# Attention and gated MLP on one core: the first MLP stage's rectified values kept in PSUM

## The chip, the cores and the metric

The kernel runs on one core of one Trainium2 chip. The metric is the device time of one execution in microseconds (us), lower is better. Engines are named as in the profile: PE is TensorE, DVE is VectorE, ACT is ScalarE, POOL is GpSimd, SP is SyncE, which issues most DMA transfers. PE writes its results to PSUM, in banks of 128 partitions by 512 fp32 values; DVE and ACT read and write both PSUM and SBUF; POOL works in SBUF here.

## The reference

Two stages follow each other. First causal attention with a decay, for 8 batches of 8 heads, 576 tokens and a head width of 64:

```python
scores = scale * np.matmul(q, k.transpose(0, 1, 3, 2))
log_f = np.log(np.clip(f, 0.0001, 1.0))
cum = np.cumsum(log_f, axis=-1)
decay = cum[:, :, :, None] - cum[:, :, None, :]
scores = np.where(causal, -1000000000.0, scores + decay)
attn = np.exp(scores - max); attn = attn / (sum + 1e-09)
x = np.matmul(attn, v)          # 8 x 8 x 576 x 64, then to 8 x 576 x 512
```

Then a gated MLP with a product over the tokens:

```python
h = np.maximum(x @ w_in, 0.0)                 # 576 x 1024 per batch
u, v = h[..., :512], h[..., 512:]
v_n = (v - mean(v)) / np.sqrt(var(v) + 1e-06)   # over the 512 columns
v_s = np.einsum('ts,bsd->btd', w_spatial, v_n) + b_spatial[None, :, None]
out = (u * v_s) @ w_out
```

## The kernel before

All matrix products run on PE with operands split in two parts, a rounded high part and the low remainder, and three products in place of one; so nearly each PSUM result is copied by ACT into a high part, and DVE or POOL subtracts it to get the low part. Only the first five pairs of heads (P < NF) use plain fp32 operands in attention.

Attention goes by pairs of heads, four pairs to a batch. For a pair and head, `scores` makes four tiles of 128 queries in PSUM (`sc`), DVE adds the mask and takes the row maximum (L338), ACT takes the exponential into `tt` (L340), POOL divides by the sum (L348). `transposes` turns `tt` by PE into `tp` tiles (L394) and `evac` writes them as high and low part into `eh` and `el` (ACT L383, DVE L384). The last 64 queries of both heads run in one tile (`scores_tail`, L359, into `tl`) and `transposes_tail` turns five blocks of keys, three in a first `tp` tile and two in a second, the fourth block and the last 64 keys. For those last 64 keys, of which 64 partitions are a second copy, the low part is wanted in partitions 64 to 127 of the high tensor: L416 copies it there from the low tensor. `attend` multiplies with `v` into `x0` and `x1`, and ACT and DVE evacuate them to `xh` and `xl` (L442, L443, L445).

`moe(b)` takes a batch. Its first stage makes the normalised half `v_n`: for five blocks of tokens, i = 0 to 4, twelve matmuls (eight for the last block, whose 64 tokens stand twice) accumulate a tile `ps` of 128 by 512. ACT rectifies it (L533) into an SBUF tile `vx`, DVE takes statistics (L534, L535), POOL adds epsilon (L536) and raises to the power -0.5 (L537), DVE subtracts the mean and scales (L538), ACT rounds to the high part `vnh` (L540) and POOL subtracts for the low part `vnl` (L542). `vx` has two buffers, and a buffer is free again after L542. For the last block, ACT first copies the lower half to `vx` (L531) and DVE adds the upper half (L532). Further stages make `u` (eight accumulations, rectified by ACT at L563), the product over the tokens (eight accumulations, gated by DVE at L582) and the output product.

The accumulators come from `acc`: in batches 0 to 6 from the pool `ps_m` with two PSUM banks, in the last batch in turn from three pools of two banks each. A bank goes to a new accumulation when the last reader of the old one is through.

What sets the order: attention and the MLP are two generators. They are advanced in turn, attention ahead by a quarter of a batch, each by its own estimated cost. A scheduler then puts the instructions in an order for each engine by their dependences and by an estimate of times; on the chip each engine takes its own list strictly in that order and waits where an operand or a bank is not ready. So a changed dependence changes the order of all five lists.

Of the kernel before, what the change touches and what calls it, by code (L numbers as in the profile page):

```python
# [12 lines left out]
AF = mybir.ActivationFunctionType  # L13
ALU = mybir.AluOpType
# [5 lines left out]
NF = 5  # L20
NQ = 4
LEAD = 0.25
S = 576
D = 64
NB = 4
# [8 lines left out]
def f32(ap):  # L34
    return ap.bitcast(F32)
# [3 lines left out]
def attn_gmlp_kernel(ctx: ExitStack, tc: tile.TileContext, qk, v, f, w_in, w_sp, b_sp, w_out, out):  # L39
# [17 lines left out]
    V, A, G, T, SY = nc.vector, nc.scalar, nc.gpsimd, nc.tensor, nc.sync  # L57
# [20 lines left out]
    lnc = cst.tile([128, 3], F32, name="lnc")  # L78
# [175 lines left out]
    ET = {"f": cst.tile([128, 2, 1600], F32, name="ef", tag="eh")}  # L254
# [3 lines left out]
    def mm(o, l, r, st, sp):  # L258
        last['mm'] = T.matmul(o, l, r, start=st, stop=sp)  # L259
        return last['mm']  # L260
# [113 lines left out]

    nev = [0]

    def evac(P, ps, sel):
        if P < NF:
            (V.tensor_copy if nev[0] % 2 == 1 else A.copy)(sel(ET["f"]), ps)
            nev[0] += 1  # L380
            return
        h_ap, l_ap = sel(ET["h"]), sel(ET["l"])
        A.copy(h_ap, ps)  # L383
        V.tensor_tensor(out=l_ap, in0=ps, in1=f32(h_ap), op=ALU.subtract)  # L384

    def transposes(P, h):
        if P == NF and h == 0:
# [12 lines left out]
    def transposes_tail(P):  # L400
        def ev(e, off, step, n):
            return e[:, :, off:off + step * n].rearrange("p h (c s) -> p c h s", s=step)[:, :, :, 0:64]
        for cs, off, step in (((0, 1, 2), 512, 512), ((4, 3), 576, 640)):
            n = len(cs)
            tp = PS['t'].tile([128, 512], F32, name="tp")
            for j, c in enumerate(cs):
                T.transpose(out=tp[:, j * 128:(j + 1) * 128], in_=tl[:, c * 128:(c + 1) * 128], identity=ident)  # L407
            pv = tp[:, 0:128 * n].rearrange("p (c h s) -> p c h s", h=2, s=64)

            def dst(e):  # L410
                st = e[:, :, off:off + 64]
                return bass.AP(tensor=st.tensor, offset=st.offset,
                               ap=[list(st.ap[0]), [step, n], list(st.ap[1]), list(st.ap[2])])
            evac(P, pv, dst)
            if P >= NF and cs[0] == 4:
                V.tensor_copy(ET["h"][64:128, :, S:640], f32(ET["l"][64:128, :, S:640]))  # L416
            yield 107 * n

    def attend(P, h, xh, xl):
# [30 lines left out]
    def attention(b, ws=None):  # L450
        for P in range(b * PPB, (b + 1) * PPB):
# [27 lines left out]
            if nxt:  # L479
                yield from scores(P + 1, 0)  # L480
            yield from transposes_tail(P)
            if P + 2 < NPAIR:
                split(P + 2)
# [16 lines left out]
    def acc(b):  # L500

        nps[0] += 1
        pool, tag = ((ps_m, "ps"), (PS["t"], "tp"), (PS["s"], "sc"))[nps[0] % 3 if b == B - 1 else 0]
        return pool.tile([128, DM], F32, name=tag)

    def moe(b):
        X = [xs.pop(b * PPB + p) for p in range(PPB)]
        vh, vl = [], []
        for i in range(NB + 1):
            ps = acc(b)  # L510
            n = 0
            for p in range(PPB):
                xh, xl = X[p]
                if i < NB:
                    t = slice(128 * i, 128 * i + 128)
                    terms = ((xh[:, t], 0), (xh[:, t], 1), (xl[:, t], 0))
                else:
                    terms = ((xh[:, TL:640], 0), (xh[:, TL:640], 1))
                for l, r in terms:
                    mm(ps, l, win[p][:, r, :], n == 0, n == len(terms) * PPB - 1)  # L520
                    n += 1
                yield 648
            th = mo.tile([128, DM], F32R, name="vnh", tag="vnh", bufs=5)
            tlo = mo.tile([128, DM], F32R, name="vnl", tag="vnl", bufs=4) if i < NB else None
            x = mo.tile([128, DM], F32, name="vx", tag="vx", bufs=2)
            st = mo.tile([128, 6], F32, name="st", tag="st", bufs=2)
            mv = mo.tile([128, 2], F32, name="mv", tag="mv", bufs=2)
            m = slice(0, 128)
            if i == NB:
                m = slice(0, 64)  # L530
                A.copy(x[64:128, :], ps[64:128, :])  # L531
                V.tensor_tensor(out=x[m, :], in0=ps[m, :], in1=x[64:128, :], op=ALU.add)  # L532
            A.activation(x[m, :], ps if i < NB else x[m, :], AF.Relu)  # L533
            V.bn_stats(out=st[m, :], in_=x[m, :])  # L534
            V.bn_aggr(out=mv[m, :], in_=st[m, :])  # L535
            G.tensor_tensor(out=mv[m, 1:2], in0=mv[m, 1:2], in1=lnc[m, 0:1], op=ALU.add)  # L536
            G.tensor_tensor(out=mv[m, 1:2], in0=mv[m, 1:2], in1=lnc[m, 1:2], op=ALU.pow)  # L537
            V.tensor_scalar(out=x[m, :], in0=x[m, :], scalar1=mv[m, 0:1], scalar2=mv[m, 1:2],  # L538
                            op0=ALU.subtract, op1=ALU.mult)
            A.copy(th[m, :], x[m, :])  # L540
            if i < NB:
                G.tensor_tensor(out=tlo, in0=x, in1=f32(th[:]), op=ALU.subtract)  # L542
                vl.append(tlo)
            else:
                A.copy(vb_[m, :], x[m, :])
                G.tensor_tensor(out=th[64:128, :], in0=x[m, :], in1=f32(th[m, :]), op=ALU.subtract)
            vh.append(th)
            yield 0
        if b == 0:
            open_m2()  # L550
        us = {}
        for j in range(NJ):
            for t0, nt in HALVES:
                ps = acc(b)
                n = 0
                for p in range(PPB):
                    xh, xl = X[p]
                    for l, r in ((0, xh), (1, xh), (0, xl)):
                        mm(ps[:, 0:nt], win[NJ + j][:, l, 128 * p:128 * p + 128], r[:, t0:t0 + nt], n == 0, n == 3 * PPB - 1)
                        n += 1  # L560
                    yield 369
                us[j, t0] = m2[0].tile([128, 320], F32, name="u", tag="U", bufs=9)
                A.activation(us[j, t0][:, 0:nt], ps[:, 0:nt], AF.Relu)  # L563
        if b % 2 == 0:
            gt[0] = m2[0].tile([128, 2, NJ, 128], F32R, name="gt", tag="gt")
        r0 = 64 * (b % 2)
        for t0, nt in HALVES:
            gh, gl = [], []
            for j in range(NJ):
                ps = acc(b)  # L570
                o = ps[:, 0:nt]
                js = slice(128 * j, 128 * j + 128)
                for c in range(NB):
                    mm(o, vh[c][:, js], sph[c][:, t0:t0 + nt], c == 0, False)
                    mm(o, vh[c][:, js], spl[c][:, t0:t0 + nt], False, False)
                    mm(o, vl[c][:, js], sph[c][:, t0:t0 + nt], False, False)
                    yield 370
                mm(o, vh[NB][:, js], spta[:, t0:t0 + nt], False, False)
                mm(o, vb_[:, js], sptb[:, t0:t0 + nt], False, True)
                yield 246  # L580
                g = us[j, t0][:, 0:nt]
                V.tensor_tensor(out=g, in0=o, in1=g, op=ALU.mult)  # L582
                gh.append(m2[0].tile([128, 320], F32R, name="gh", tag="GH", bufs=3))
                gl.append(m2[0].tile([128, 320], F32R, name="gl", tag="U", bufs=9))
                A.copy(gh[j][:, 0:256], g[:, 0:256])  # L585
                G.tensor_tensor(out=gl[j][:, 0:256], in0=g[:, 0:256], in1=f32(gh[j][:, 0:256]), op=ALU.subtract)  # L586
                if t0:
                    th, tlo = (gt[0][:, r, j, r0:r0 + 64] for r in range(2))
                    A.copy(th, g[:, 256:320])
                    G.tensor_tensor(out=tlo, in0=g[:, 256:320], in1=f32(th), op=ALU.subtract)  # L590
            for c0 in (0, 128):
                yield from w_out_tile(b, [g[:, c0:c0 + 128] for g in gh], [g[:, c0:c0 + 128] for g in gl],
                                      [(b, t0 + c0, 0, 128)])
        if b % 2 == 1:
            yield from w_out_tile(b, *[[gt[0][:, r, j, :] for j in range(NJ)] for r in range(2)],
                                  [(b - 1, TL, 0, 64), (b, TL, 64, 64)])
# [50 lines left out]
    def open_m2():  # L647
        while need[0] != "m2":
            need[0] = next(wgen)
        late.close()  # L650
        m2.append(ctx.enter_context(tc.tile_pool(name="m2", bufs=1, reuse_waits="tile")))
        last["m2"] = None
        converted()
# [54 lines left out]
```

## Time and profile before

| what | value |
|---|---|
| time, median of 3 runs (lowest to highest) | 806.53 us (804.21 to 806.70) |
| time of the profiled execution | 803.75 us |
| its span in the profile | 802.0 us |
| granted TensorE clock, mean | 0.991 |
| instructions | 15504 |

The profile is of one execution. Busy time of an engine is time in which one of its instructions runs; the chain that ended last is found by going back from the last instruction to what released it. A group of instructions is given as line, engine, operation, out<-in with shapes, count, then busy us and mean ns of one, then the engine's idle time before it and what ended most of that. A stretch is given as from:to in us, its length, then PE, PE weight loads, DVE, ACT and POOL busy with counts, the granted clock, the share and rate of DMA. A line of the timeline is start, duration, engine, line, operation, tiles, and in brackets the engine's idle time just before it with what ended it. A wait is given as who waited and for whom, with its sum in us, the times, and the longest.

### The profile page before, as it was taken

The page shows a single profiled execution, that of the slowest core. Times are in us where ns is not written, and L with a number is a line of the kernel's source. Part 1 is how long each engine was busy: PE and PEld are TensorE (multiplying, and loading weights), DVE is VectorE, ACT ScalarE, POOL GpSimd, SP SyncE. Part 2 cuts the span into 40 slices and gives each one's busy share as a digit, 9 for nine tenths or more (in the row PEclk, how much of TensorE's full clock was granted, in tenths as well). Part 3 has the DMA queues.
Part 4 walks back from the last instruction along what each step waited for, and adds up shares of the span by engine and source line. Part 5 has one row for each costly group of instructions (what it writes and reads, how often), then busy time and mean ns, then how long its engine had stood idle before and what let it go on. Part 6 is the DMA issues. An engine that isn't in the chain of part 4 may idle for free.

```text
span 802.0 us, 15504 instructions
## 1 busy us (share of the span) xinstructions
PE 781.6 (97%) x4980; PEld 703.8 (88%) x4981; DVE 553.2 (69%) x1665; ACT 535.6 (67%) x1418; POOL 475.2 (59%) x660
## 2 busy tenths in 40 slices
PE   8997989989999999999999999999999999999997
PEld 4776879879899989989899989999899988999996
DVE  7887786985768768676776669666787558674421
ACT  7785677676777767766676668766687667664431
POOL 5775796766765548655656647555776447643251
PEclk9998999999999999999999999999999999999999
DMA  8839645564454664545545455564555464330001
GB/s 222 251 95 236 173 131 135 137 165 137 122 126 102 164 172 114 126 118 135 136 112 141 117 144 128 144 158 133 145 126 136 118 166 126 83 78 14 27 1 66
DMA packets 41713, 103.48 MB, mean 129 GB/s; under 512 B 6831, under 2 KB 8879, under 8 KB 41568
## 3 DMA queue, kind: packets, MB, share of 16 engines
q1 hardware_dynamic: 41306, 101.96, 49.6%
q8 instruction: 40, 0.66, 0.3%
q10 hardware_dynamic: 326, 0.53, 0.3%
q14 instruction: 41, 0.34, 0.1%
HBM read 39.42 MB, written 10.68 MB: 62 GB/s over the span
## 4 chain that ended last, share of the span: by engine, by line
PE 86%; POOL 4%; ACT 3%; DMA 2%; issue 2%; DVE 2%; POOLq 0%; ACTq 0%; DVEq 0%
PE ps L259 46%; PE sc L259 16%; PE x L259 13%; PE tp L394 8%; PE tp L259 2%; PE tp L407 2%; POOL tt L348 1%; POOL lo L279 1%; DMA tb<-lo 1%; DMA vraw<-in_dram 1%; ACT eh L383 1%; ACT tt L340 1%; POOL wa L171 0%; DMA out_dram<-o 0%; DMA ft<-in_dram 0%
## 5 line engine op out<-in xcount | busy, mean ns | idle before, releaser
L348 POOL TENSOR_SCALAR tt<-tt,sm 128x128 f32<-128x128 f32 (+3 forms) x256 | 141.9, 574 | 78.7 <-DVE sm L344 61.2
L338 DVE CUSTOM_DVE_ANT_0 tt<-sc,zm 128x128 f32<-128x128 f32 (+3 forms) x256 | 122.7, 486 | 91.4 <-PE tp L394 65.1
L383 ACT CAST eh<-tp 128x512 fp32r<-128x512 f32 (+1 forms) x270 | 111.3, 425 | 76.3 <-PE tp L394 50.1
L340 ACT ACTIVATE tt<-tt,nm 128x128 f32<-128x128 f32 (+3 forms) x256 | 144.3, 565 | 22.7 <-DVE nm L338 21.2
L384 DVE TENSOR_TENSOR el<-tp,eh 128x512 fp32r<-128x512 f32 (+1 forms) x270 | 126.7, 484 | 25.5 <-ACT eh L383 23.1
L394 PE MATMUL tp<-ident,tt 128*128 128x128 f32 x640 | 111.6, 279 | 3.2 <-DVE el L384 3.1
L259 PE MATMUL sc<-ta 128*128 128x128 f32 (+1 forms) x336 | 108.8, 330 | 1.9 <-DVE nm L338 1.6
L259 PE MATMUL sc<-tb 68*128 68x128 f32 (+1 forms) x336 | 105.8, 319 | 3.0 <-DMA tb<-lo 3.0
L259 PE MATMUL x<-eh,vt 128*128 128x320 f32 (+4 forms) x378 | 102.7, 286 | 0.4 <-POOL vt L315 0.4
L259 PE MATMUL ps<-xh,win 128*128 128x256 f32 (+1 forms) x464 | 99.0, 303 | 0.4 <-ACT u L563 0.3
L586 POOL TENSOR_TENSOR gl<-u,gh 128x256 fp32r<-128x256 f32 x64 | 47.3, 740 | 87.4 <-ACT gh L585 77.9
L279 POOL TENSOR_TENSOR lo<-raw,hi 128x640 fp32r<-128x640 f32 (+1 forms) x56 | 83.6, 1514 | 14.8 <-ACT hi L277 14.4
L259 PE MATMUL ps<-win,xh 128*128 128x512 f32 x296 | 91.6, 398 | 0.0
L259 PE MATMUL x<-el,vt 128*128 128x256 f32 x324 | 90.7, 304 | 0.2 <-DVE el L384 0.2
L394 PEld LDWEIGHTS tp<-ident,tt 128*128 128x128 f32 x640 | 76.5, 141 | 12.2 <-issue 2.3
L442 ACT CAST xh<-x 64x256 fp32r<-64x256 f32 (+1 forms) x128 | 49.7, 394 | 48.6 <-PE x L259 46.3
L259 PEld LDWEIGHTS ps<-xh,win 128*128 128x128 f32 x464 | 75.9, 191 | 2.1 <-ACT u L563 0.9
L259 PEld LDWEIGHTS x<-eh,vt 128*128 128x128 f32 x378 | 71.2, 189 | 3.3 <-POOL vt L315 1.0
L259 PE MATMUL ps<-sph,vnh 128*128 128x256 f32 (+1 forms) x240 | 73.2, 305 | 0.7 <-ACT o L611 0.7
L259 PE MATMUL ps<-wo,gh 128*128 128x512 f32 x224 | 72.1, 407 | 0.7 <-ACT wo L172 0.5
L443 DVE TENSOR_TENSOR xl<-x,xh 64x256 fp32r<-64x256 f32 (+1 forms) x128 | 57.5, 452 | 21.4 <-ACT xh L442 18.6
L259 PE MATMUL ps<-sph,vnl 128*128 128x256 f32 (+1 forms) x240 | 71.7, 299 | 0.0
(178 smaller groups left out, 1919.8 us busy)
## 6 DMA issues: line engine op xcount, KB each, us to landing
raw<-in_dram SPq DMA_DIRECT2D x28, 608.0 KB
ta<-hi SPq DMA_DIRECT2D x56, 304.0 KB
vraw<-in_dram SPq DMA_DIRECT2D x32, 320.0 KB
tb<-hi SPq DMA_DIRECT2D x56, 160.0 KB
ta<-lo SPq DMA_DIRECT2D x56, 160.0 KB
out_dram<-o SPq DMA_DIRECT2D x32, 256.0 KB
ta<-hi SPq DMA_DIRECT2D x56, 144.0 KB
tb<-lo SPq DMA_DIRECT2D x56, 144.0 KB
```

The lines of the kernel that those rows point to most:

```text
L259: last['mm'] = T.matmul(o, l, r, start=st, stop=sp)
L279: G.tensor_tensor(out=lo[:, c], in0=raw[:, c], in1=f32(hi[:, c]), op=ALU.subtract)
L338: V.tensor_tensor_reduce(out=t, in0=sc[:, 0:n], in1=zm[:, 640 - n:640], scale=-0.125, scalar=3.0e38, op0=ALU.add, op1=ALU.min, accum_out=n ...
L340: last["exp"] = last["exp", P, h, i] = A.activation(t, t, AF.Exp, bias=nm[:, i:i + 1], scale=-1.0, accum_out=se[:, i, 0:1])
L348: G.tensor_scalar(out=t, in0=t, scalar1=sm[:, i:i + 1], scalar2=1.0, op0=ALU.mult, op1=ALU.mult)
L383: A.copy(h_ap, ps)
L384: V.tensor_tensor(out=l_ap, in0=ps, in1=f32(h_ap), op=ALU.subtract)
L394: T.transpose(out=tp[:, (i - c) * 128:(i - c + 1) * 128], in_=tt[h][:, TOFF[i] + 128 * c:TOFF[i] + 128 * c + 128], identity=ident)
L407: T.transpose(out=tp[:, j * 128:(j + 1) * 128], in_=tl[:, c * 128:(c + 1) * 128], identity=ident)
L442: last[P, h] = A.copy(hi, ps[m0:m0 + 64, 0:n])
L443: V.tensor_tensor(out=lo, in0=ps[m0:m0 + 64, 0:n], in1=f32(hi), op=ALU.subtract)
L586: G.tensor_tensor(out=gl[j][:, 0:256], in0=g[:, 0:256], in1=f32(gh[j][:, 0:256]), op=ALU.subtract)
```

## The change

Three edits. First, in the MLP's first stage the rectified values are written back into the PSUM accumulator; statistics and normalisation read them there, and only the normalised values go to the SBUF tile `vx`. With it the bank's last reader is the normalisation, and the `vx` buffer is first written there and no longer by the Relu. Second, epsilon is added by DVE with a constant in place of POOL with a column of constants. Third, of the second tile of `transposes_tail` the fourth block's low part is subtracted into `el` as before, and that of the last keys is subtracted in place in partitions 64 to 127 of `eh`, so that L416 falls away; the first 64 partitions' low part of the last keys, which nothing reads, is no longer made.

```diff
-    def evac(P, ps, sel):
+    def evac(P, ps, sel, last_keys=False):
...
         A.copy(h_ap, ps)
-        V.tensor_tensor(out=l_ap, in0=ps, in1=f32(h_ap), op=ALU.subtract)
+        if last_keys:
+            V.tensor_tensor(out=l_ap[:, 1], in0=ps[:, 1], in1=f32(h_ap[:, 1]), op=ALU.subtract)
+            V.tensor_tensor(out=h_ap[64:128, 0], in0=ps[64:128, 0], in1=f32(h_ap[64:128, 0]), op=ALU.subtract)
+        else:
+            V.tensor_tensor(out=l_ap, in0=ps, in1=f32(h_ap), op=ALU.subtract)
...
-            evac(P, pv, dst)
-            if P >= NF and cs[0] == 4:
-                V.tensor_copy(ET["h"][64:128, :, S:640], f32(ET["l"][64:128, :, S:640]))
+            evac(P, pv, dst, cs[0] == 4)
...
-                V.tensor_tensor(out=x[m, :], in0=ps[m, :], in1=x[64:128, :], op=ALU.add)
-            A.activation(x[m, :], ps if i < NB else x[m, :], AF.Relu)
-            V.bn_stats(out=st[m, :], in_=x[m, :])
+                V.tensor_tensor(out=ps[m, :], in0=ps[m, :], in1=x[64:128, :], op=ALU.add)
+            A.activation(ps[m, :], ps[m, :], AF.Relu)
+            V.bn_stats(out=st[m, :], in_=ps[m, :])
             V.bn_aggr(out=mv[m, :], in_=st[m, :])
-            G.tensor_tensor(out=mv[m, 1:2], in0=mv[m, 1:2], in1=lnc[m, 0:1], op=ALU.add)
+            V.tensor_scalar(out=mv[m, 1:2], in0=mv[m, 1:2], scalar1=1.0e-6, scalar2=None, op0=ALU.add)
             G.tensor_tensor(out=mv[m, 1:2], in0=mv[m, 1:2], in1=lnc[m, 1:2], op=ALU.pow)
-            V.tensor_scalar(out=x[m, :], in0=x[m, :], scalar1=mv[m, 0:1], scalar2=mv[m, 1:2],
+            V.tensor_scalar(out=x[m, :], in0=ps[m, :], scalar1=mv[m, 0:1], scalar2=mv[m, 1:2],
```

In the changed file the first stage's Relu is L535, the statistics L536 and L537, the added epsilon L538, the power L539, the normalisation L540, and the last keys' two subtractions are L385 and L386.

The lists of the engines change with it. On PE, in batch 2's first stage, the third accumulation (ps_4020) follows the second (ps_3950) in the program before so; tp and sc, x0 and x1 are attention's transposes, scores and products with `v`:

```order
L259 MATMUL ps_3950<-win3_572,xh_3389 128x512 x2
L259 MATMUL ps_3950<-win3_572,xl_3390 128x512
L259 MATMUL x1_3830<-el_1228,vt_3551 128x192
L259 MATMUL x1_3830<-eh_1227,vt_3551 128x64
L394 MATMUL tp_3899<-ident_70,tt0_67 128x128 x3
L259 MATMUL ps_4020<-win0_235,xh_2417 128x512 x2
L259 MATMUL ps_4020<-win0_235,xl_2418 128x512
L259 MATMUL ps_4020<-win1_398,xh_2716 128x512 x2
L259 MATMUL sc_3932<-ta_3865 128x384
L259 MATMUL sc_3932<-tb_3866 128x384
```

Five matmuls of attention stand between the two, and the third accumulation is itself broken by scores. In the changed program the rows ahead of the third accumulation are these, and the second's last row is followed by three single matmuls (two of scores, one into x0) before they begin:

```order
L259 MATMUL sc_3811<-ta_3562 128x512
L259 MATMUL sc_3811<-tb_3563 128x512
L398 MATMUL tp_3776<-ident_70,tt1_68 128x128 x2
L259 MATMUL x0_3829<-el_1228,vt_3551 128x256
L259 MATMUL x0_3829<-eh_1227,vt_3551 128x128
L398 MATMUL tp_3784<-ident_70,tt1_68 128x128
L259 MATMUL x0_3829<-el_1228,vt_3551 128x128
L259 MATMUL x1_3830<-eh_1227,vt_3551 128x320
L259 MATMUL x1_3830<-el_1228,vt_3551 128x320
L259 MATMUL x1_3830<-eh_1227,vt_3551 128x320
L259 MATMUL x1_3830<-el_1228,vt_3551 128x320
L259 MATMUL ps_4020<-win0_235,xh_2417 128x512 x2
```

Fifteen matmuls of attention now stand between the two accumulations, and each accumulation runs unbroken. On DVE, the second group's statistics and normalisation (vx_4009, mv_4011) stood before among attention's evacuations like this:

```order
L534 BN_STATS st_4010<-vx_4009 128x6
L443 TENSOR_TENSOR xl_3714<-x1_3830,xh_3713 64x320
L535 BN_AGGR mv_4011<-st_4010 128x2
L445 TENSOR_TENSOR xl_3714<-x1_3830,xl_3714 64x320
L384 TENSOR_TENSOR el_1228<-tp_3899,eh_1227 128x384
L338 ISA tt0_67,nm_3917<-sc_3932,zm_77 128x384
L338 ISA nm_3917 128x1
L538 TENSOR_SCALAR vx_4009<-vx_4009,mv_4011 128x512
```

In the changed program the same group's end stands so on DVE, with the third group's statistics right behind the normalisation:

```order
L537 BN_AGGR mv_4011<-st_4010 128x2
L388 TENSOR_TENSOR el_1228<-tp_3776,eh_1227 128x256
L388 TENSOR_TENSOR el_1228<-tp_3784,eh_1227 128x128
L445 TENSOR_TENSOR xl_3714<-x0_3829,xh_3713 64x256
L538 TENSOR_SCALAR mv_4011<-mv_4011 128x1
L343 TENSOR_REDUCE sm_3789<-se0_107 128x4
L447 TENSOR_TENSOR xl_3714<-x0_3829,xl_3714 64x256
L344 RECIPROCAL sm_3789<-sm_3789 128x4
L540 TENSOR_SCALAR vx_4009<-ps_3950,mv_4011 128x512
L536 BN_STATS st_4071<-ps_4020 128x6
```

The epsilon row is new on DVE and the normalisation reads the accumulator ps_3950.

## The prediction

> **What bounds the kernel now.** I read the page first, for the busy shares and the chain that ended last; then the waits of TensorE; then busy time by stretch; then the groups by line and shape; last the timeline around the edited lines.
>
> ```profile
> span 802.0 us, 15504 instructions
> PE 781.6 (97%) x4980; PEld 703.8 (88%) x4981; DVE 553.2 (69%) x1665; ACT 535.6 (67%) x1418; POOL 475.2 (59%) x660
> PE 86%; POOL 4%; ACT 3%; DMA 2%; issue 2%; DVE 2%; POOLq 0%; ACTq 0%; DVEq 0%
> ```
>
> TensorE (PE) is busy for 97% of the span and carries 86% of the chain; it idles 802.0 - 781.6 = 20.4 us in all. The edit removes no matmul, so it can only move what lies in those 20.4 us, or add to them. Where they lie is told by stretches (after each engine's busy time, the granted clock):
>
> ```profile
> 80.00:130.00 50.00, 47.85 (x279) 41.49 (x278) 36.81 (x107) 34.17 (x86) 41.81 (x50) 0.97 0.59 157
> 130.00:200.00 70.00, 65.97 (x425) 59.19 (x424) 55.00 (x162) 49.64 (x135) 46.11 (x58) 0.98 0.54 138
> 410.00:470.00 60.00, 60.00 (x407) 56.31 (x406) 38.83 (x125) 38.22 (x107) 29.24 (x44) 1.00 0.55 144
> 775.00:802.00 27.00, 21.96 (x115) 18.91 (x113) 3.78 (x8) 5.02 (x14) 7.12 (x12) 0.98 0.14 49
> 290.00:320.00 30.00, 30.00 (x186) 27.14 (x186) 24.54 (x68) 22.17 (x56) 18.91 (x28) 1.00 0.50 125
> ```
>
> The first batch's MLP (80 to 130) leaves 2.2 us idle, the next stretch 4.0, the end 5.0. In the middle nothing is left: 60.00 of 60.00, and also 30.00 of 30.00 in 290 to 320, which is a first MLP stage, the part that is edited. There TensorE starts a matmul every 30.00 / 186 = 0.161 us. Of TensorE's waits, those that VectorE ended are the ones that this change can shorten:
>
> ```profile
> PE tp L394 <- DVE el L384: 3.1, 3, 2.1
> PE sc L259 <- DVE nm L338: 1.6, 4, 0.8
> PE tp L407 <- DVE el L384: 0.8, 1, 0.8
> ```
>
> Together 5.5 us. No row has the Relu (L533) or the normalisation (L538) as releaser: the stage's chain is today fully covered.
>
> **The parts on VectorE and GpSimd.** The rows of the edited lines, and of the nearest operations, by shape:
>
> ```profile
> L538 DVE TENSOR_SCALAR vx<-vx,mv 128x512 f32<-128x512 f32 x32 | 21.8, 683 | 5.1 <-POOL mv L537 4.2
> L538 DVE TENSOR_SCALAR vx<-vx,mv 64x512 f32<-64x512 f32 x8 | 7.1, 890 | 3.2 <-POOL mv L537 3.2
> L534 DVE BATCH_NORM_STATS2 st<-vx 128x6 f32<-128x512 f32 x32 | 21.6, 686 | 6.2 <-ACT vx L533 6.1
> L384 DVE TENSOR_TENSOR el<-tp,eh 128x512 fp32r<-128x512 f32 x54 | 37.1, 686 | 6.8 <-ACT eh L383 6.1
> L384 DVE TENSOR_TENSOR el<-tp,eh 128x256 fp32r<-128x256 f32 x81 | 33.9, 418 | 7.7 <-ACT eh L383 7.4
> L384 DVE TENSOR_TENSOR el<-tp,eh 128x128 fp32r<-128x128 f32 x54 | 15.2, 282 | 3.2 <-ACT eh L383 3.1
> L416 DVE CAST eh<-el 64x128 fp32r<-64x128 f32 x27 | 10.8, 400 | 0.9
> L365 DVE TENSOR_SCALAR sm<-sm 128x1 f32<-128x1 f32 x32 | 4.8, 149 | 4.8 <-ACT tl L364 4.3
> L536 POOL TENSOR_TENSOR mv<-mv,lnc 128x1 f32<-128x1 f32 x32 | 6.7, 214 | 49.3 <-DVE mv L535 30.6 <-DVE sm L343 18.7
> L536 POOL TENSOR_TENSOR mv<-mv,lnc 64x1 f32<-64x1 f32 x8 | 1.5, 182 | 6.6 <-DVE mv L535 4.1 <-DVE sm L344 2.4
> L533 ACT ACTIVATE vx<-ps 128x512 f32<-128x512 f32 x29 | 17.1, 597 | 7.9 <-POOL vnl L542 4.0 <-PE ps L259 3.8
> ```
>
> Last keys: 27 pairs lose a 128x256 subtraction (418 ns) and the copy (400) and get two subtractions of 128 columns, one on 64 partitions; both at the 128x128 row, 282. That is 27 x (818 - 564) = 6.9 us less VectorE time. Epsilon: 40 additions leave GpSimd (6.7 + 1.5 = 8.2 us) and come to VectorE at L365's 149 ns: 40 x 0.149 = 6.0 us more. It also takes one hand-over between engines out of the chain, since the addition now follows the aggregation on the same engine.
>
> Normalisation from PSUM: no tensor_scalar of that shape from PSUM is in the trace. The bounds are L538's own best, 518 ns, and L384's 686, which reads PSUM for the same 512 columns; the second is nearer and I take it.
>
> ```profile
> L538 DVE TENSOR_SCALAR vx<-vx,mv x40: 518/547/1897, 99.1 to 769.3; 128x512 f32<-128x512 f32 x32, 64x512 f32<-64x512 f32 x8
> 303.60 3.15 POOL L279 TENSOR_TENSOR lo<-raw,hi 128x640 fp32r<-128x640 f32 x2
> 303.67 1.79 DVE L538 TENSOR_SCALAR vx<-vx,mv 128x512 f32<-128x512 f32 x1 [0.17 <-POOL mv L537]
> ```
>
> An undisturbed L538 gets slower by 686 - 547 = 0.14 us, but the source view's maximum of 1897 ns, and the 1.79 us beside a long GpSimd subtraction, show what it suffers today; if that goes with the second operand in PSUM, 40 x 0.686 = 27.4 us stand against today's 21.8 + 7.1 = 28.9. So between +5.6 and -1.5 us; I take -1.5. The Trainium skill, "VectorE: DVE Perf Modes", section "Why PSUM operands drop a tier", says that the doubled fp32 rate needs both SBUF read ports and that PSUM offers one, which speaks against this part of the change: by it the 0.14 us is the whole story, and VectorE's sum would be 5.6 us up on this line. The trace agrees as far as its undisturbed rows go (547 against 686).
>
> Statistics from PSUM: L534 already takes 686, the same as a PSUM read of that width, so zero, 0.1 us either way. The Relu's destination: no ScalarE row that writes PSUM exists; L533's 597 is the nearest, 0.1 us either way, 40 x 0.1 = 4 us on an engine that is 67% busy. VectorE in sum: -6.9 + 6.0 - 1.5 = -2.4 us of 553; GpSimd -8.2 of 475. None of this is on TensorE, and matmuls cover it; what can come through is the stretch from 130 to 200, where VectorE is busy 55.00 of 70 and ends TensorE's waits: 27 pairs over some 690 us put 2.7 pairs there, 2.7 x 0.254 = 0.7 us. I credit -0.7.
>
> **The part on TensorE: the bank is held longer.** This is the term that counts. Today an accumulation's bank is free after the Relu; afterwards only after the normalisation, with GpSimd's power in between. Two banks serve the stage, so accumulation i+2 waits for the normalisation of i. Batch 2's first group, from its last matmul to the third group's first:
>
> ```profile
> 293.55 0.39 PE L259 MATMUL ps<-win,xl 128*128 128x512 f32 x1
> 294.78 0.58 ACT L533 ACTIVATE vx<-ps 128x512 f32<-128x512 f32 x1
> 297.30 0.56 POOL L537 TENSOR_TENSOR mv<-mv,lnc 128x1 f32<-128x1 f32 x1
> 297.89 0.60 DVE L538 TENSOR_SCALAR vx<-vx,mv 128x512 f32<-128x512 f32 x1
> 299.64 0.71 PE L259 MATMUL ps<-win,xh 128*128 128x512 f32 x2
> ```
>
> The chain takes 298.49 - 293.94 = 4.55 us and the third group comes 5.7 us after the first: it would fit even unmoved. A long case, batch 4's fourth group:
>
> ```profile
> 483.09 0.48 PE L259 MATMUL ps<-win,xl 128*128 128x512 f32 x1
> 487.13 0.60 ACT L533 ACTIVATE vx<-ps 128x512 f32<-128x512 f32 x1 [1.34 <-POOL vnl L542]
> 494.04 0.55 DVE L538 TENSOR_SCALAR vx<-vx,mv 128x512 f32<-128x512 f32 x1
> ```
>
> Here it takes 494.59 - 483.57 = 11.0 us. The new order answers by moving attention matmuls in between. Counted in it, from the end of one accumulation to the start of the next but one: 48, 44, 35 and 53 matmuls for batch 2's first four groups (38, 22, 24 and 27 before), the same four counts for batch 4, and 30 as the least in any batch. At 0.161 us each that is 7.7, 7.1, 5.6 and 8.5 us, and 4.8 at the least. The short chain is covered with 3 us to spare; the long one is late by 11.0 - 8.5 = 2.5 us. But 1.34 us of it was the Relu waiting until GpSimd had released the SBUF tile (row above), and in the change the Relu writes no such tile: 1.2 us remain. That SBUF wait is not abolished: it moves to the normalisation on VectorE, with the score reductions and evacuations queued behind it, and transposes and scores wait for those; it lies some 3 us later in the chain, by when GpSimd is through, so I cost it at zero (1.34 us a time if not).
>
> One group late in this way in all seven gated batches together makes +1.2 us. The sum against the profiled execution's own time: 803.75 + 1.2 - 0.7 = 804.25 us. That execution lies 806.53 - 803.75 = 2.78 us under the median of the runs shown, so the forecast on the median's footing is 807.0 us, within 0.3% (2.4 us, about what a measurement of this kernel can tell from no change).
>
> **Rivals.** Slower: the long chain is the rule, not the exception, and TensorE stands at the third accumulation for VectorE in every batch. Price: 1.2 us in each of the seven gated batches (the eighth takes its accumulators from three pools in turn), 8.4 us, so 803.75 + 8.4 = 812.15, or 814.9 on the median's footing. It decides where a chain outlasts its cover, which is 4.8 us at the least. For it: VectorE, ScalarE and GpSimd take their queues in order, and 11.0 us is no freak where all three are loaded. Against it: today's Relu gate of the same sort costs no idle time. The Trainium skill, "PSUM — Partial Sum Buffer", section "Summary: rules for kernel authors", says to evacuate promptly because PSUM is tight; by that rule this rival is the case. The trace has nothing yet to show for it: 30.00 of 30.00 us busy in the stage.
>
> Faster: the new interleaving removes VectorE's waits around the first batch. The largest, the VectorE instruction ahead of it, and the stretch after it with the clock:
>
> ```profile
> 111.45 1.67 DVE L166 SCALAR_TENSOR_TENSOR w<-w,wa 128x512 uint32<-128x512 uint32 x1
> 114.51 0.56 PE L394 MATMUL tp<-ident,tt 128*128 128x128 f32 x2 [2.13 <-DVE el L384]
> ```
>
> ```profile
> 115.00:119.00 4.00, 3.98 (x17) 3.61 (x17) 3.94 (x12) 3.81 (x10) 4.00 (x4) 0.62 0.00 0
> ```
>
> The wait of 2.13 us is followed by 4 us at a granted clock of 0.62, worth 4 x 0.38 = 1.5 us. If all 5.5 us go and this with them, 7.0 us are won: 796.75, or 799.5 on the median's footing. For it: the evacuation that came late stands behind a step of the weight conversion (L166, 1.67 us) on VectorE, and VectorE gets lighter. Against it: at that place the new program has as much on VectorE, with an epsilon more.
>
> The change does nothing on the chip: everything stays under TensorE, 806.5 us. It reads the same as the forecast and adds to its chance.
>
> **How the numbers follow.** Forecast 0.44 (within 0.3% for 0.38 of it, 0.03 on each side), inert 0.04, slower rival 0.27, faster rival 0.25. Hence faster 0.28, same 0.42, slower 0.30. Signs are mixed: the likeliest case's own range is 804.6 to 809.4, the 2.4 us either way. For eight in ten the range goes to both rivals' prices and stops just inside: 800 to 814.
>
> **What would show it.** In the changed profile TensorE's waits should list at most 1 to 3 us with the new normalisation line as releaser; a sum of 6 us or more means the slower rival. The stage around 290 to 320 should stay fully busy. VectorE should be at about 551 us and GpSimd at 467; the new normalisation near 686 ns with no outlier above 1 us; the copy of last keys gone. If the wait near 114 us and the slow clock behind it are gone, the faster rival holds. I am wrong if the time leaves 804.6 to 809.4 with neither in the rows, for instance through a changed end after 775 us.

## The result and the profile after

The changed kernel takes 810.05 us (median of 10 executions, 807.97 to 812.75), the kernel before in the same session 805.16 us (median of 10, 803.58 to 806.7). The ratio is 1.0062, with a 95% interval from 1.0049 to 1.0075: slower by 0.6%, some 5 us. The profiled execution took 809.76 us with a span of 807.8 us, against 803.75 and 802.0 before.

The page of the changed kernel, first the span, then the busy times:

```profile
span 807.8 us, 15502 instructions
PE 783.4 (97%) x4980; PEld 701.8 (87%) x4981; DVE 549.2 (68%) x1705; ACT 538.0 (67%) x1418; POOL 466.3 (58%) x620
```

TensorE is still the bound. Of the span's 5.8 us it was busy 1.8 us longer (783.4 - 781.6) and idle 4.0 us longer (24.4 against 20.4). GpSimd lost 8.9 us and VectorE 4.0, and neither bought time. Waits of TensorE in the changed kernel (releaser, sum in us, times, longest); two rows of 1.2 us from the kernel's start are left out:

```profile
PE x L259 <- DMA vraw<-in_dram: 3.2, 2, 2.2
PE sc L259 <- DVE nm L338: 3.1, 6, 1.6
PE sc L259 <- DMA tb<-lo: 2.6, 1, 2.6
PE sc L259 <- DMA tb<-rows_d: 2.6, 2, 1.3
PE tp L398 <- DVE el L388: 2.0, 6, 0.5
PE ps L259 <- DVE vx L540: 0.8, 2, 0.6
```

The new normalisation (L540) is in the list, but with 0.8 us. The wait for a score reduction (L338) doubled from 1.6 to 3.1 us, a wait for a load (`tb<-rows_d`) is new, and the wait for `el` fell from 3.9 us (3.1 and 0.8) to 2.0. Where TensorE's idle time lies is read from three stretches and the end; here is the kernel before (span in us, then its length, busy time and count of PE, PEld, DVE, ACT and POOL, granted clock, DMA share, GB/s):

```profile
0.00:80.00 80.00, 72.92 (x343) 51.29 (x345) 65.38 (x208) 58.27 (x152) 52.70 (x75) 0.96 0.77 201
80.00:200.00 120.00, 113.82 (x702) 100.67 (x701) 91.81 (x268) 83.81 (x220) 87.93 (x108) 0.97 0.56 146
200.00:775.00 575.00, 572.91 (x3826) 532.88 (x3825) 392.20 (x1184) 388.45 (x1035) 327.45 (x466) 1.00 0.47 119
```

The same stretches of the changed kernel, its end, and two shorter stretches of it:

```profile
0.00:80.00 80.00, 70.36 (x336) 49.31 (x338) 65.44 (x206) 57.62 (x149) 54.73 (x77) 0.98 0.76 203
80.00:200.00 120.00, 116.97 (x738) 105.07 (x738) 94.68 (x287) 89.02 (x230) 85.58 (x103) 0.99 0.57 150
200.00:775.00 575.00, 568.27 (x3748) 522.62 (x3748) 384.25 (x1202) 385.36 (x1024) 317.58 (x429) 1.00 0.47 118
775.00:807.80 32.80, 27.84 (x164) 24.75 (x162) 4.87 (x10) 6.03 (x16) 8.38 (x13) 0.99 0.12 41
80.00:130.00 50.00, 49.10 (x289) 42.07 (x290) 39.64 (x117) 37.27 (x95) 39.54 (x44) 1.00 0.62 164
290.00:320.00 30.00, 29.37 (x184) 26.00 (x183) 24.64 (x83) 23.83 (x62) 18.49 (x24) 1.00 0.62 156
```

From 80 to 200 TensorE's idle time fell from 6.2 to 3.0 us and its clock there rose from 0.97 to 0.99. That part became faster: by 200 us 738 matmuls were done in this stretch, 36 more than before. From 200 to 775, where before only 2.1 of 575 us were idle, it is now 6.7 us, and 78 matmuls fewer are done. The gain is given back, and more. The stretch up to 80 is idle for 9.6 us against 7.1, but in the experiments below that give TensorE one and the same order this idle time alone lies anywhere from 7.1 to 9.1 us; how much of the 2.5 us is the change's is not settled. Of the span's 5.8 us, then, some 1.5 us are the balance of the two later stretches, 2.5 us lie ahead of 80 us, and 1.8 us are busy time.

An early place where something is given back shows the held bank. The timeline of the changed kernel, batch 1's first stage (start, duration, engine, line, operation, the wait ahead of it in brackets):

```profile
196.57 0.39 PE L259 MATMUL ps<-win,xl 128*128 128x512 f32 x1
197.31 0.58 ACT L535 ACTIVATE ps<-ps 128x512 f32<-128x512 f32 x1
199.25 0.15 DVE L538 TENSOR_SCALAR mv<-mv 128x1 f32<-128x1 f32 x1
199.50 2.06 POOL L348 TENSOR_SCALAR tt<-tt,sm 128x128 f32<-128x128 f32 x4 [10.70 <-DVE mv L538]
201.52 0.55 POOL L539 TENSOR_TENSOR mv<-mv,lnc 128x1 f32<-128x1 f32 x1
203.12 0.81 DVE L540 TENSOR_SCALAR vx<-ps,mv 128x512 f32<-128x512 f32 x1
203.99 0.72 PE L259 MATMUL ps<-win,xh 128*128 128x512 f32 x2 [0.63 <-DVE vx L540]
```

From the last matmul to the end of the normalisation it takes 203.93 - 196.96 = 7.0 us. Some 2 us of it the power waits on GpSimd behind four of attention's scalings, and some 1 us the normalisation waits in VectorE's queue. TensorE then stands for 0.63 us. That is the longest such wait in the kernel.

### The profile page after: what moved, and what is told of

Its sections match the earlier page's. It is cut to its first block, busy times and chain, and to the rows that moved or that the text cites. A ratio compares the mean times of both kernels' runs of the same rounds, so it can differ in the third digit from the quotient of the medians.

```text
span 807.8 us, 15502 instructions
## 1 busy us (share of the span) xinstructions
PE 783.4 (97%) x4980; PEld 701.8 (87%) x4981; DVE 549.2 (68%) x1705; ACT 538.0 (67%) x1418; POOL 466.3 (58%) x620
## 4 chain that ended last, share of the span: by engine, by line
PE 85%; DVE 5%; DMA 4%; ACT 3%; issue 2%; POOL 1%; SPq 0%; ACTq 0%; POOLq 0%; DVEq 0%
PE ps L259 45%; PE sc L259 15%; PE x L259 13%; PE tp L398 8%; PE tp L259 2%; PE tp L411 2%; DMA vraw<-in_dram 2%; DVE tt L338 1%; DMA tb<-lo 1%; DMA tb<-rows_d 1%; DVE el L388 1%; POOL tt L348 1%; ACT tt L340 1%; ACT hi L277 1%; DVE xl L445 0%
## 5 line engine op out<-in xcount | busy, mean ns | idle before, releaser
L348 POOL TENSOR_SCALAR tt<-tt,sm 128x128 f32<-128x128 f32 (+3 forms) x256 | 139.1, 562 | 74.7 <-DVE sm L344 30.4
L338 DVE CUSTOM_DVE_ANT_0 tt<-sc,zm 128x128 f32<-128x128 f32 (+3 forms) x256 | 122.7, 485 | 82.2 <-PE tp L398 62.8
L388 DVE TENSOR_TENSOR el<-tp,eh 128x384 fp32r<-128x384 f32 (+3 forms) x243 | 116.8, 491 | 28.0 <-ACT eh L383 25.5
L259 PE MATMUL ps<-xh,win 128*128 128x256 f32 (+1 forms) x464 | 97.1, 302 | 0.1
L279 POOL TENSOR_TENSOR lo<-raw,hi 128x640 fp32r<-128x640 f32 (+1 forms) x56 | 83.2, 1506 | 16.9 <-ACT hi L277 16.6
L259 PE MATMUL ps<-wo,gh 128*128 128x512 f32 x224 | 74.2, 405 | 0.0
L259 PEld LDWEIGHTS sc<-ta 128*128 128x128 f32 x336 | 64.2, 191 | 11.2 <-DVE nm L338 5.7
```

The source lines that it names most:

```text
L279: G.tensor_tensor(out=lo[:, c], in0=raw[:, c], in1=f32(hi[:, c]), op=ALU.subtract)
L338: V.tensor_tensor_reduce(out=t, in0=sc[:, 0:n], in1=zm[:, 640 - n:640], scale=-0.125, scalar=3.0e38, op0=ALU.add, op1=ALU.min, accum_out=n ...
L348: G.tensor_scalar(out=t, in0=t, scalar1=sm[:, i:i + 1], scalar2=1.0, op0=ALU.mult, op1=ALU.mult)
```

## The experiments

Theory 1: the bank that is held until the normalisation costs the time. Theory 2: the three parts make the scheduler give TensorE another order of the same matmuls, and it is the order that costs. "The order of before" means below that each matmul is tied behind the one that stood ahead of it in the kernel before, so that TensorE's list is the same matmul for matmul; the other engines' lists are made by the same scheduler as ever, so they are not those of the kernel that the order came from, and no run holds their share apart. The tie is:

```diff
+    for a, b in zip(at, at[1:]):
+        tc.add_manual_dep(T.made[b].ins, T.made[a].ins.name, mybir.DependencyInfo(
+            mybir.DependencyClass.NoSync, mybir.DependencyReason.DATA), reason="order")
```

In such a kernel the line numbers are 17 higher and matmuls are recorded at L42, transposes at L46. All ratios are to runs of the kernel before on the same chip.

**One part alone, order free.** The PSUM part alone:

```diff
-            A.activation(x[m, :], ps if i < NB else x[m, :], AF.Relu)
-            V.bn_stats(out=st[m, :], in_=x[m, :])
+            A.activation(ps[m, :], ps[m, :], AF.Relu)
+            V.bn_stats(out=st[m, :], in_=ps[m, :])
...
-            V.tensor_scalar(out=x[m, :], in0=x[m, :], scalar1=mv[m, 0:1], scalar2=mv[m, 1:2],
+            V.tensor_scalar(out=x[m, :], in0=ps[m, :], scalar1=mv[m, 0:1], scalar2=mv[m, 1:2],
```

> Only the first edit: rectified values stay in PSUM; epsilon and last keys as before. If the bank that is held longer is the cause (theory 1), this kernel is slower than the one before by as much as the whole change, 1.004 to 1.008, with TensorE's waits for the normalisation in its profile. If any edit only reshuffles the engines' orders and the loss comes from that (theory 2), it lies anywhere from 0.995 to 1.006 and need not be near 1.006. If the two other edits are the cause, it is within 0.998 to 1.002.

The epsilon alone:

```diff
-            G.tensor_tensor(out=mv[m, 1:2], in0=mv[m, 1:2], in1=lnc[m, 0:1], op=ALU.add)
+            V.tensor_scalar(out=mv[m, 1:2], in0=mv[m, 1:2], scalar1=1.0e-6, scalar2=None, op0=ALU.add)
```

> Only the second edit: epsilon added by VectorE. Theory 1: 0.998 to 1.002, since no bank is held longer. Theory 2: a reshuffled order of its own, anywhere from 0.995 to 1.006.

The last keys alone (the first and second hunk of the diff above), and both of these together:

> Only the third edit: last keys' low part subtracted in place. Theory 1: 0.997 to 1.001, a little gain at most from 6.9 us less on VectorE. Theory 2: anywhere from 0.995 to 1.006.

> The second and third edits without the first. Theory 1: 0.997 to 1.001, so the change less its PSUM part is no slower than before. Theory 2: not predictable from the two single runs, anywhere from 0.995 to 1.006; a ratio that is not the sum of the single ones speaks for it.

Measured: PSUM part 1.0148 (1.0125 to 1.0171), epsilon 1.0191 (1.017 to 1.0212), last keys 1.0052 (1.0032 to 1.0071), epsilon with last keys 1.0179 (1.0154 to 1.0204). Two of the parts alone are much slower than all three together, and forty additions of one column cost 15 us. Nor do they add up: 0.5 + 1.9 + 1.5 = 3.9% against 0.62%. Costs that hang on the operations alone should not shrink when the parts are put together. Three of the four ratios lie above every range that was expected, under either theory; only the last keys lie inside one. With the PSUM part alone TensorE waits only 0.5 us for the normalisation, so it is not by such waits that this kernel loses 1.5%. The waits of TensorE that grew most with the epsilon alone:

```profile
PE sc L259 <- DVE nm L338: 4.6, 8, 1.1
PE ps L259 <- ACT o L611: 2.8, 3, 1.1
PE x L259 <- POOL vt L315: 2.2, 1, 2.2
```

None of them, and no other row, is for the edited line. They are waits of attention's and the output's matmuls for work that the edit doesn't touch.

**Operations and order crossed.** The whole change in the order of before:

> The whole change, but TensorE's list forced to the order of the kernel before, matmul for matmul; the other engines' lists are free. Held bank (theory 1): with only 22 to 38 matmuls of cover, 3.5 to 6.1 us at 0.161 us each, against chains of 4.6 to 8.7 us, TensorE waits 1 to 2 us at most third accumulations, so 1.015 to 1.04, and the normalisation heads the list of TensorE's waits with 15 to 30 us. Order alone (theory 2): the loss came with the new order, so with the old one it is gone: 0.997 to 1.002.

The kernel before, with no operation changed, in the changed kernel's order:

> The kernel before with TensorE's list forced to the order of the changed kernel; nothing else is changed. Theory 2 (the new order costs it): 1.004 to 1.008, as the whole change. Theory 1 (the waits for the held bank cost it, which are absent here): 0.998 to 1.002. Between them, 1.002 to 1.004, means a share for each.

| | operations of before | all three parts |
|---|---|---|
| TensorE in the order of before | 1 | 1.0523 (1.0501 to 1.0545) |
| TensorE in the changed kernel's order | 1.0168 (1.015 to 1.0187) | 1.0062 (1.0049 to 1.0075) |

Both theories have their part, and both new ratios lie above the ranges that were expected. In the order of before the whole change costs 41 us (847.01 against 805.71). TensorE is idle 31.3 us longer there (51.7 against 20.4) and busy 10.6 us longer (792.2 against 781.6), at a mean clock of 0.980 against 0.991. Its waits for the normalisation, 23.5 us, are the largest part and lie inside the 15 to 30 us that were expected:

```profile
PE ps L42 <- DVE vx L557: 21.5, 13, 3.7
PE sc L42 <- DVE vx L557: 2.0, 1, 2.0
```

One of them in its timeline (two groups of a stage side by side):

```profile
593.64 0.62 PE L42 MATMUL ps<-win,xl 128*128 128x512 f32 x2
596.31 1.07 ACT L552 ACTIVATE ps<-ps 128x512 f32<-128x512 f32 x2
597.55 1.29 DVE L553 BATCH_NORM_STATS2 st<-ps 128x6 f32<-128x512 f32 x2
599.63 1.07 POOL L556 TENSOR_TENSOR mv<-mv,lnc 128x1 f32<-128x1 f32 x2 [0.22 <-DVE mv L555]
600.72 1.52 DVE L557 TENSOR_SCALAR vx<-ps,mv 128x512 f32<-128x512 f32 x2
601.58 0.91 PE L42 MATMUL ps<-win,xh 128*128 128x512 f32 x2 [3.62 <-DVE vx L557]
```

TensorE stands for 3.62 us while Relu, statistics, power and normalisation run one after the other. It starts at 601.58, inside the row of two normalisations, so it seems to need the first bank only. In the changed kernel's own order the same waits come to 0.8 us. But that order has a price of its own: with the old operations, which hold nothing longer, it costs 1.7%. The largest row of TensorE's waits there:

```profile
PE sc L42 <- DVE nm L355: 6.8, 7, 2.1
```

Two of these seven are 2.13 us long, at 407 and at 599 us. The second, on GpSimd, VectorE and at TensorE:

```profile
595.23 3.10 POOL L296 TENSOR_TENSOR lo<-raw,hi 128x640 fp32r<-128x640 f32 x2
595.29 1.78 DVE L555 TENSOR_SCALAR vx<-vx,mv 128x512 f32<-128x512 f32 x1 [0.55 <-POOL mv L554]
...
598.16 0.68 DVE L355 CUSTOM_DVE_ANT_0 tt<-sc,zm 128x512 f32<-128x512 f32 x1
598.90 0.59 PE L42 MATMUL sc<-ta 128*128 128x288 f32 x1 [2.13 <-DVE nm L355]
```

The scores wait for a reduction (L355) that stands on VectorE, an addition of the same stage and an evacuation in between, behind a normalisation from SBUF of 1.78 us, one of the outliers. At 407 us it is the same, behind one of 1.80 us. The 4 us behind the two waits ran at a reduced clock (the third number from the end):

```profile
407.05:411.05 4.00, 4.00 (x18) 4.00 (x19) 2.95 (x9) 1.28 (x3) 2.48 (x6) 0.60 0.60 125
598.90:602.90 4.00, 4.00 (x18) 3.98 (x18) 2.37 (x9) 1.27 (x3) 1.89 (x5) 0.57 0.55 116
```

In the changed kernel the scores wait 0.28 and 0.27 us at the same two places (404.38 and 593.88 us), the clock behind them is full, and no normalisation takes over 0.81 us. The two places are therefore worth some 2 x (1.85 + 4 x 0.41) = 7.0 us. That is most of what separates the two kernels of the lower row (1.68 - 0.62 = 1.06%, 8.5 us), as far as one profiled execution of each can tell: at these places the slower but steady normalisation from PSUM is the better one. Of each 1.85 us the normalisation itself explains 1.0 (1.8 against 0.81); the rest lies in what stands around it on VectorE.

**The epsilon, crossed likewise.** The epsilon alone in the order of before, and the kernel before in the epsilon kernel's order:

> Epsilon added by VectorE, with TensorE's list forced to the order of the kernel before. If the 1.9% of this edit alone came from the order that it got: 0.998 to 1.003. If it came from the operation (VectorE's queue is later, GpSimd's power is later): 1.012 to 1.020 again.

> The kernel before with TensorE's list forced to the order that the epsilon edit alone got. Order: 1.013 to 1.022. Operation: 0.998 to 1.003.

Measured 1.0032 (1.0018 to 1.0046) and 1.0327 (1.0303 to 1.0351). Of the epsilon's 1.9%, then, 0.3% is left when the order of before is kept. The order by itself costs more than the whole, 3.3%, and more than the 1.3 to 2.2% that were expected of it; so the two do not simply add.

**The parts in the order of before.** With the tie as above:

> The kernel before with the first part of the change alone (the rectified first-stage values stay in the PSUM bank for statistics and normalisation), and TensorE held to the kernel before's order, matmul for matmul. Theory 1 (a bank that is held until the normalisation has read it leaves an order made for a short hold too little cover): ratio 1.03 to 1.06, with 15 to 30 us of TensorE waits for the normalisation, as the whole change in the old order had 23.5 us and 1.0523. Theory 2 (what counts is only which order TensorE gets, the hold itself costs little): at most 1.01, with under 5 us of such waits; the same part in its own new order measured 1.0148.

> The kernel before with the third part of the change alone (the low part of the last keys is subtracted in place, 27 VectorE instructions 254 ns shorter each), and TensorE held to the kernel before's order. Theory 2 (order): the 0.5 % that this part lost in its own order goes, ratio 0.995 to 1.001, since nothing but shorter VectorE work is left; 0.995 if some of the 5.5 us of TensorE waits for VectorE shrink with it. Against it, if the subtraction in place itself costs (it holds a buffer longer or comes later): 1.004 or more, as in its own order (1.0052).

> The kernel before with the second and third part of the change (epsilon on VectorE, last keys' low part in place) and TensorE held to the kernel before's order. Theory 2 (order): the 1.8 % of the two parts in their own order goes; ratio 0.997 to 1.004, between the third part alone and the second part alone (1.0032) in the old order. If the operations themselves cost when they are together: 1.01 or more.

| parts | order free | order of before |
|---|---|---|
| last keys | 1.0052 (1.0032 to 1.0071) | 1.0008 (0.9997 to 1.002) |
| epsilon and last keys | 1.0179 (1.0154 to 1.0204) | 1.0022 (1.0009 to 1.0035) |
| PSUM part | 1.0148 (1.0125 to 1.0171) | 1.0594 (1.0562 to 1.0627) |

The first two lose nearly all of their cost when the order is kept: theory 2 for them. The tie itself should therefore cost hardly more than the last keys' 0.1%, unless that part gains what the tie costs; the kernel before, tied to its own order, was not run. The PSUM part goes the other way: theory 1 for it, at the upper end of what was expected. Its waits, in the order of before:

```profile
PE ps L42 <- DVE vx L555: 25.9, 14, 3.7
PE sc L42 <- DVE vx L555: 2.1, 1, 2.1
```

The last keys in the order of before were the candidate for a kernel faster than the one before. Its VectorE time fell by 553.2 - 548.9 = 4.3 us, and its time stayed the same. TensorE's waits for `el` there:

```profile
PE tp L46 <- DVE el L405: 4.0, 5, 2.1
```

The long one of 2.1 us is still there: what delays it is not what the edit shortens. No version measured here is faster than the kernel before.

**The order alone, changed a little.** No operation is changed, only a number of the planner:

```diff
-LEAD = 0.25
+LEAD = 0.27
```

> No operation is changed: only one number of the planner by which the order of the work is made is moved a little (LEAD to 0.27), so that it gives TensorE another order of the same matmuls. Theory 2 (an order that wasn't chosen by trial costs some tenths of a per cent to some per cent, whatever the operations): ratio 1.003 to 1.03. If orders that the planner makes are alike in time, so that the losses of the parts have to come from their operations: 0.997 to 1.003.

Measured 1.0019 (1.0008 to 1.003). That lies below theory 2's 1.003 and inside the range for orders that are alike in time. Theory 2 in its strong form falls: a new order does not always cost some tenths of a per cent or more. How far this order departs from that of before was not set beside the other orders, so it may cost little because it moved little. Its idle time from 200 to 775 us is 3.7 us (2.1 before). What makes one order cost 0.2% and another 1.7 to 3.3% is not told by these runs beyond the waits shown above.

## Why the prediction was right in part and wrong in part

The time, 810.05 us, lies in the stated range of 800 to 814, but not in the likeliest case's own range of 804.6 to 809.4, and the ratio is outside the 0.3% that this case allowed. Point by point:

- **Bound.** Right in the main: TensorE is busy for 97% and no matmul goes. But of the 5.8 us of span only 4.0 are idle time; 1.8 are busy time, for which the prediction had no term.
- **Last keys.** Right in price: 27 x (818 - 281 - 295) ns = 6.5 us, by the medians of the source views of the changed kernel, against 6.9. The copy's 400 ns is a mean with outliers in it (median 233, most 1207), and in the order of before VectorE's total fell by 4.3 us only. The credit of 0.7 us on TensorE was not found: in the order of before this part gains nothing.
- **Epsilon.** Right in price: 146 ns each, 5.8 us in all. GpSimd came to 466.3 us (467 foretold).
- **Normalisation from PSUM.** Wrong, and outside the bounds of 518 to 686 ns. The source view of the changed kernel (ns: least, median, most; first and last start):

```profile
L540 DVE TENSOR_SCALAR vx<-ps,mv x37: 768/805/812, 98.5 to 772.7; 128x512 f32<-128x512 f32 x29, 64x512 f32<-64x512 f32 x8
L535 ACT ACTIVATE ps<-ps x37: 567/582/592, 90.7 to 770.3; 128x512 f32<-128x512 f32 x29, 64x512 f32<-64x512 f32 x8
L536 DVE BATCH_NORM_STATS2 st<-ps x37: 680/694/700, 94.1 to 770.9; 128x6 f32<-128x512 f32 x29, 64x6 f32<-64x512 f32 x8
L538 DVE TENSOR_SCALAR mv<-mv x40: 114/146/157, 96.9 to 771.8; 128x1 f32<-128x1 f32 x32, 64x1 f32<-64x1 f32 x8
```

  Three more, in the last batch, are listed under other tiles, at 808 to 810 ns. At 805 ns the 40 take 32.2 us, 3.3 more than the 28.9 of before, where 1.5 less were foretold. The neighbour that I took, a subtraction from PSUM, has no per-partition scalars; the operation differed, and only the place of its operand was alike. Right was that the outliers go: 812 ns at most, against 1897. Relu and statistics were priced rightly (582 against 597, 694 against 686). The Trainium skill, "VectorE: DVE Perf Modes", section "Why PSUM operands drop a tier", says that a PSUM operand costs fp32 its doubled rate; the trace agrees in direction, with 805 against 547 ns.
- **VectorE in sum.** 549.2 us, 551 foretold, but not for the reasons given: the three edited parts come to -6.5 + 5.8 + 3.3 = +2.6 us, and the page's total fell by 4.0. In the order of before the whole change has 557.0 us of VectorE, and 1.9 us of the difference between before and after lie in a step of the weight conversion that nobody edited, L166 (11.3 and 9.4 us, the same 12 instructions). The sum agreed by chance.
- **The held bank.** Right: 0.8 us of waits stand against the 1.2 that I gave it, and chains of 7.0 us fit between the short one of 4.55 and the long one of 11.0. The stage from 290 to 320 stayed nearly full (29.37 of 30 us), and what is idle there is no wait for the normalisation. The slower rival, this wait in every batch, did not come. It is what happens when the order does not cover the hold (1.0523, and 1.0594 for the PSUM part alone). The rule of the Trainium skill, "PSUM — Partial Sum Buffer", section "Summary: rules for kernel authors", to evacuate promptly, holds in those two runs and not in the changed kernel, where matmuls put in between cover the hold.
- **The faster rival.** Half of it came. The wait near 114 us fell from 2.13 to 0.54 us, and the clock from 80 to 130 rose from 0.97 to 1.00. The prediction had this and the slower time as separate cases; a gain from 80 to 200 us and a larger loss behind it came together. That the two nearly cancel, and the time so lies only 3 us above the forecast of 807.0, is luck.
- **The step that failed** is "The new order answers by moving attention matmuls in between": the moved matmuls were counted as cover and priced at nothing. Moving them costs, 1.68% with the old operations. In the changed kernel some now wait for what feeds them: the loads of two tables and the score reductions. The timeline of its longest wait after 200 us, with the last load's issue on SyncE's queue:

```profile
506.45 0.30 PE L259 MATMUL sc<-ta 128*128 128x128 f32 x1 [0.62 <-DMA ta<-hi]
...
507.11 0.38 SPq L304 DMA_DIRECT2D tb<-rows_d  x1
...
508.03 0.30 PE L259 MATMUL sc<-tb 68*128 68x128 f32 x1 [1.29 <-DMA tb<-rows_d]
```

  The last load is issued at 507.11 and its scores stand for 1.29 us for it. The kernel before has no wait for a load after 80 us; with its operations in the changed kernel's order there is one again at this place, 0.74 us at 511.82, so it belongs to the order. With 0.63 us for the normalisation at 203.99 these are 2.5 of the 6.7 us that TensorE is idle from 200 to 775 (2.1 before); the rest are waits under 0.6 us each.

What stays open: TensorE's busy time also grew where the order was free (789.2 us with the epsilon alone against 781.6, 7.6 of that kernel's 16.5 us of span). Matmuls and weight loads are the same in number there; the runs don't say what takes longer. Nor was it tried which of the moved matmuls costs the order its 1.7%.

## What to carry to other kernels

Where a scheduler makes the order, an edit's price has two parts, and they are measured apart: the new operations in the old order, and the old operations in the new order. A buffer that is held longer costs little where the order has enough work to put in between (0.8 us of waits) and a lot where it has not (23.5 us), but the work that is put in between must have its own inputs ready earlier, which is one place to look for the bill. Price an operation by a row with the same operation and the same scalars, and not by one that only reads the same memory.

## What the runs showed of the hardware

A normalisation of 128x512 fp32 with two per-partition scalars takes 805 ns from PSUM and 547 ns from SBUF; from PSUM it hardly varies (768 to 812), from SBUF some take up to 1897. The eight from SBUF in the kernel before that took over 0.7 us all ran beside a GpSimd instruction of L279, L315, L371 or L542 (so did the one shown above, beside L296). In the changed kernel normalisations from PSUM ran beside the same GpSimd work in 0.79 to 0.81 us.

A long TensorE wait can cost more than itself, because the granted clock behind it is lower for some microseconds. The first three stretches of 4 us lie right behind waits of 2.03, 2.61 and 3.62 us of the whole change in the order of before, the fourth behind a wait of 1.44 us with the PSUM part alone, the fifth behind one of 2.18 us with the epsilon alone, both with the order free (the clock is the number before the last two):

```profile
121.27:125.27 4.00, 3.50 (x21) 2.90 (x21) 3.94 (x8) 3.98 (x11) 3.23 (x2) 1.00 0.15 31
324.56:328.56 4.00, 4.00 (x20) 3.98 (x21) 1.72 (x5) 1.55 (x3) 2.80 (x4) 0.62 0.59 131
601.58:605.58 4.00, 4.00 (x11) 3.14 (x12) 0.67 (x1) 1.22 (x2) 3.63 (x4) 0.57 0.88 249
598.31:602.31 4.00, 3.85 (x18) 3.67 (x19) 2.05 (x9) 2.54 (x9) 3.90 (x5) 0.64 0.39 106
121.98:125.98 4.00, 4.00 (x31) 4.00 (x32) 3.59 (x13) 2.19 (x7) 4.00 (x3) 1.00 0.70 185
```

Where the clock fell it was 0.57 to 0.64 for 4 us, worth another 4 x 0.4 = 1.6 us each. No one length of wait divides the two cases here: 1.44 us were enough in one place, and 2.18 us were not in another. Every wait of 2.3 us or more after 80 us in the traces of this case, thirteen in all, is followed by 4 us at 0.50 to 0.68. The Trainium skill, "TensorE: Matmul & The Clock Gate", section "What's actually happening", puts the fall of the clock at an idle window of about 3.4 us; here single waits of 2.61 us, of 2.13 us in the kernel before and of 1.44 us with the PSUM part alone were enough, so 3.4 us is not the least wait to reckon with.
